# Attention units in pairs on TensorE, and both softmaxes of a pair scaled at the head of the next step

## The chip, the cores and the metric

One core of one Trainium2 chip. The metric is the device time of one execution of the program in microseconds; the table of the profile section gives it for the kernel before.

## What is computed

From the reference, cut to the core:

```python
def _attn_ref(q, k, v):            # (4, 8, 576, 64): batch, heads, positions, head size
    scores = scale * np.matmul(q, k.transpose(0, 1, 3, 2))
    ...                            
    scores = np.where(masks, scores, -1e9)   # heads 0-3: the last 32 positions; heads 4-7: every 4th of the last 128
    attn = np.exp(scores - np.max(scores, axis=-1, keepdims=True))
    attn = attn / (np.sum(attn, axis=-1, keepdims=True) + 1e-09)
    return np.matmul(attn, v)

def reference(**kwargs):
    x = attention output as (2304 tokens, 512)
    h = x @ w_in                   # (512, 2048)
    r = np.maximum(h, 0.0)
    x = (s * (r * r) + b) @ w_out  # (2048, 512)
    h = x @ moe2_w_in
    return (h * np.cos(h)) @ moe2_w_out
```

## The kernel before

The 2304 tokens are cut into five tiles of 384, 384, 512, 512 and 512 tokens. Each tile goes through the first MLP and later through the second. The loop at L539 counts steps p: 16 steps for each tile and MLP (one chunk of 128 of the 2048 hidden channels each), 160 in all. In step p, `mm_in` (L317) makes the hidden chunk h(p) on TensorE, `relu2` (L385) or `cos1` to `cos_split` turn it into g(p) on ScalarE and VectorE, and `mm_out` (L334) adds g(p-2) of an earlier step into the four outputs y. Tile 0 of the first MLP uses plain fp32 weights; every other tile uses each operand as a high and a low part, three matmuls of the rounded type in place of one.

Attention runs in 48 units (192 positions of two heads each; `dil` units have 4 blocks of 80 keys, plain ones 3 blocks of 96). Eight units (tile 0) run ahead of the loop. The other 40 run inside the steps of the first MLP, one tile ahead of the one that needs them: units 8 to 15 in steps 3 to 14, 16 to 27 in steps 15 to 30, 28 to 39 in steps 31 to 46, 40 to 47 in steps 48 to 62. A unit has five stations:

- `a_scores` (L211): 3 or 4 matmuls (`sc`) into one PSUM bank,
- `a_softmax` (L227): on VectorE scale and mask (L236) and the row maximum (L245), then on ScalarE 3 or 4 exponentials with their sums (L248),
- `a_norm` (L254): on VectorE 1/sum (L259, L260) and the scaling of the weights (L261),
- `a_transpose` (L263): transposes on TensorE (`tp`), copied to SBUF by ScalarE (L271),
- `a_pv` (L274): 6 or 8 small matmuls with v (`pv`), copied to the MLP's input by ScalarE (L299).

The order of all engines is written by hand (`manual_schedule`): every engine does its instructions in the order in which the loop records them. `at((p, phase), f)` puts a station into step p: phase 0 stands right behind `mm_in`, phases 1 and 2 at the step's end. Of each unit, with p counting one unit a step in most steps:

```python
at((p, 0), lambda i=i: a_scores(i, ps_a))
at((p, 1), lambda i=i: a_softmax(i))
at((p + 1, 0), lambda i=i: a_norm(i))
at((p + 2, 2), lambda i=i: a_transpose(i, ps_a, nc.scalar.copy))
at((p + 4, 0), lambda i=i: a_pv(i, ps_a))
```

h, sc, tp and pv share four PSUM banks in turn (pool `ps_a`): each waits until the tile four places earlier in that order has been read. The tiles of q and k, of v, and the softmax tiles have two buffers each.

In the same steps both MLPs' weights are prepared. `w_float` on ScalarE (L115, L116) and `w_join` on VectorE (four operations, L122 to L131) turn a chunk of 64-bit words into fp32: two chunks a step in steps 0 to 14 for the first MLP, and from step 19 on some 4, 8 and 10 chunks a tile for the second (`at((p, ph), ...)` at L517 to L532), each followed by `w_cut` (L141) one step later. `w_split` (L133) makes the high and low parts of the first MLP's weights, two a step in steps 16 to 28. Loads are issued from SyncE's queue, in the order of the program.

Of the kernel before, what the change touches and what calls it, by code (L numbers as in the profile page):

```python
# [26 lines left out]
NTILE = len(SIZES)  # L27
T = max(SIZES)
NCC = DM // P
NFC = DFF // P  # L30
LAG = (2, 3)
W_FIRST, W_STEPS = (7, 8, 9, 10), {8: 1, 9: 2, 11: 3}
V_LATE = 3
AHEAD = 3
WPRE, W_PACE = 4, 2.0
IN_CUT = 13

# [15 lines left out]
def attention_then_two_mlps(ctx, tc, qk_p, qk_d, v_p, v_d, mask_p, mask_d, w1, w2, sv, bv, out):  # L53
    nc = tc.nc
# [9 lines left out]
    ps_a = pool("ps_a", 4, space=PSUM)  # L64
# [13 lines left out]
    def xy_tile(t):  # L78

        if t not in xy:  # L80
            place = late[0] if t == 2 else xypool
            xy[t] = place.tile([P, NCC, T], F32, tag=f"xy{t % 3}", name=f"xy{t}")[:, :, : SIZES[t]]
        return xy[t]
# [87 lines left out]
    units = [(tb, hp) for b in blocks for hp in range(4) for tb in b]  # L171
    first_unit = [4 * sum(len(b) for b in blocks[:t]) for t in range(NTILE + 1)]
# [22 lines left out]
    def a_load(i):  # L195
        tb, hp = units[i]
        b, u = divmod(tb, 3)
        dil = hp >= 2
        nb, nq, nk = (4, DB, DK) if dil else (3, PB, PK)
        kw = nb * nk if dil else 3 * PB + WINDOW  # L200
        qk = io.tile([P, 384 + kw], F32, tag="qk", name=f"qk{i}")
        nc.sync.dma_start(qk, (qk_d if dil else qk_p)[b, hp % 2, u])
        st[i] = dict(q=qk[:, :384], k=qk[:, 384:], dil=dil, nb=nb, nq=nq, nk=nk, tb=tb, hp=hp, b=b, u=u)

    def a_load_v(i):
        d = st[i]
        vv = iov.tile([d["nk"], d["nb"], P], F32, tag="v", name=f"v{i}")
        nc.sync.dma_start(vv, (v_d if d["dil"] else v_p)[d["b"], d["hp"] % 2, d["u"]])
        d["v"] = vv

    def a_scores(i, ps):  # L211
        d = st[i]
        nb, nq, nk, dil = d["nb"], d["nq"], d["nk"], d["dil"]
        nr = 2 * nq
        acc = ps.tile([P, 512], F32, tag=ps_tag[ps.name], name=f"sc{i}")
        for j in range(nb):
            k0 = j * nk if dil else j * PB
            nc.tensor.matmul(  # L218
                acc[:nr, j * nk : (j + 1) * nk],
                d["q"][:, j * nr : (j + 1) * nr],  # L220
                d["k"][:, k0 : k0 + nk],
                start=True,
                stop=True,
            )
        d["acc"] = acc

    def a_softmax(i):  # L227
        d = st[i]
        nb, nq, nk, dil, acc = d["nb"], d["nq"], d["nk"], d["dil"], d.pop("acc")
        nr = 2 * nq  # L230
        sm = d["place"](3, [nr, nb, nk]) if "place" in d else ap_.tile([nr, nb, nk], F32, tag="sm", name=f"sm{i}")
        if dil:
            mask = m_d[:, (0 if d["u"] == 0 else 1) : (1 if d["u"] == 0 else 2), :].to_broadcast([nr, nb, nk])
        else:
            mask = m_p if d["u"] == 0 else m_p[:, 1:2, :].to_broadcast([nr, nb, nk])
        nc.vector.scalar_tensor_tensor(  # L236
            out=sm,
            in0=acc[:nr, : nb * nk].rearrange("p (j k) -> p j k", j=nb),
            scalar=1.0 / math.sqrt(D),
            in1=mask,  # L240
            op0=ALU.mult,
            op1=ALU.add,
        )
        nmax = ap_.tile([nr, nb], F32, tag="nmax", name=f"nmax{i}")
        nc.vector.tensor_reduce(out=nmax, in_=sm, op=ALU.max, axis=AX.X, negate=True)  # L245
        ssum = ap_.tile([nr, nb], F32, tag="ssum", name=f"ssum{i}")
        for j in range(nb):
            nc.scalar.activation(  # L248
                out=sm[:, j, :], in_=sm[:, j, :], func=AF.Exp, bias=nmax[:, j : j + 1], scale=1.0,
                accum_out=ssum[:, j : j + 1],  # L250
            )
        d["sm"], d["ssum"] = sm, ssum

    def a_norm(i):  # L254
        d = st[i]
        nb, nq, nk = d["nb"], d["nq"], d["nk"]
        nr = 2 * nq
        rec = ap_.tile([nr, nb, 1], F32, tag="rec", name=f"rec{i}")
        nc.vector.tensor_scalar_add(d["ssum"], d["ssum"], 1e-9)  # L259
        nc.vector.reciprocal(out=rec[:, :, 0], in_=d["ssum"])  # L260
        nc.vector.tensor_tensor(out=d["sm"], in0=d["sm"], in1=rec.to_broadcast([nr, nb, nk]), op=ALU.mult)  # L261

    def a_transpose(i, ps, copy=None):  # L263
        d = st[i]
        nb, nq, nk = d["nb"], d["nq"], d["nk"]
        nr = 2 * nq
        acc = ps.tile([P, 512], F32, tag=ps_tag[ps.name], name=f"tp{i}")
        for j in range(nb):
            nc.tensor.transpose(acc[:nk, j * nr : (j + 1) * nr], d["sm"][:, j, :], ident[:nr, :nr])  # L269
        pt = d["place"](4, [nk, 384]) if "place" in d else ap_.tile([nk, 384], F32, tag="pt", name=f"pt{i}")  # L270
        (copy or nc.vector.tensor_copy)(pt, acc[:nk, :384])  # L271
        d["pt"] = pt

    def a_pv(i, ps, tag=None):  # L274
        d = st.pop(i)
        nb, nq, nk, tb, hp = d["nb"], d["nq"], d["nk"], d["tb"], d["hp"]
        acc = ps.tile([P, 512], F32, tag=tag or ps_tag[ps.name], name=f"pv{i}")
        for j in range(nb):
            for h in range(2):
                c0 = (2 * j + h) * nq  # L280
                nc.tensor.matmul(  # L281
                    acc[h * D : (h + 1) * D, j * nq : (j + 1) * nq],
                    d["v"][:, j, h * D : (h + 1) * D],
                    d["pt"][:, c0 : c0 + nq],
                    start=True,
                    stop=True,
                )
        for t in range(NTILE):
            lo, hi = max(STARTS[t], tb * UB), min(STARTS[t + 1], tb * UB + UB)
            if lo >= hi:  # L290
                continue
            dst = xy_tile(t)[:, hp, lo - STARTS[t] : hi - STARTS[t]]
            lo, hi = lo - tb * UB, hi - tb * UB
            if d["dil"]:
                dst = dst.rearrange("p (i c) -> p c i", c=DIL)
                src = acc[:, :UB].rearrange("p (c i) -> p c i", c=DIL)[:, :, lo // DIL : hi // DIL]
            else:
                src = acc[:, lo:hi]
            nc.scalar.copy(dst, src)  # L299
# [129 lines left out]
    with tc.manual_schedule():  # L429
        n0 = 8  # L430
# [3 lines left out]
        def w_load_to(n):  # L434
            while wq[0] < min(n, 2 * NFC):
                w_load(0, wq[0], stage.tile([P, DM], I64, tag=f"s{wq[0] % 5}", name=f"stage{wq[0]}"))
                wq[0] += 1

        def w_whole(n):
# [3 lines left out]
            while q[2] < n:  # L443
# [5 lines left out]
                q[2] += 1  # L449
            w_load_to(q[2] + 1 + AHEAD)  # L450

# [4 lines left out]
        for i in range(1, n0 + V_LATE):  # L456
# [8 lines left out]
                nc.sync.dma_start(b_sb, bv.to_broadcast([P, 1]))  # L465
            if i in W_FIRST:
                w_load_to(wq[0] + 1)
        a_load(n0)
        a_load(n0 + 1)
        for k in range(n0 + 4):  # L470
            if k < n0:
                a_scores(k, ps_a)
# [13 lines left out]
        def at(slot, f):  # L486
            events.setdefault(slot, []).append(f)

        for i in range(n0, len(units)):
            t = next(t for t in range(NTILE) if i < first_unit[t + 1])  # L490
            n, j = first_unit[t + 1] - first_unit[t], i - first_unit[t]
            p = (t - 1) * NFC + (((3, 4, 5, 6, 7, 8, 9, 10) if t == 1 else (0, 1, 3, 4, 6, 8, 9, 10))[j] if n == 8 else j - 1)
            at((p, 0), lambda i=i: a_scores(i, ps_a))
            at((p + 1, 1), lambda i=i: a_load_v(i))
            if i + 2 < len(units):
                at((p, 0), lambda i=i: a_load(i + 2))
            at((p, 1), lambda i=i: a_softmax(i))
            at((p + 1, 0), lambda i=i: a_norm(i))
            at((p + 2, 2), lambda i=i: a_transpose(i, ps_a, nc.scalar.copy))
            at((p + 4, 0), lambda i=i: a_pv(i, ps_a))  # L500
        NP = 2 * NTILE * NFC

        def where(p):
            m, r = divmod(p, NTILE * NFC)
            t, fc = divmod(r, NFC)
            return m, t, fc
# [11 lines left out]
        for t, n in enumerate(BG):  # L518
            for i in range(n):
                b = t * NFC + (2 if t == 1 else 0) + (i + 0.5) * (NFC - (2 if t == 1 else 0)) / n  # L520
                p, ph = int(b), 1 + int(b % 1 >= 0.5)
# [17 lines left out]
        for p in range(NP + LAG[1]):  # L539
            if p < NP:  # L540
                m, t, fc = where(p)
# [133 lines left out]
```

## Time and profile before

| | |
|---|---|
| median of 3 runs | 934.41 us (932.59 to 934.5) |
| the profiled execution | 934.18 us, of which its span is 932.4 us |
| TensorE matmul busy | 906.8 us (97%) |
| VectorE busy | 590.2 us (63%) |
| ScalarE busy | 503.0 us (54%) |
| mean granted TensorE clock | 0.987 of full speed |
| median time to landing: q and k of a unit, v of a unit | 3.1 to 3.4 us, 2.5 to 2.7 us |

A step is read from the start of its first h matmul to that of the next step's. Steps 3 to 15 stand between 43.43 and 133.12 us of the span, steps 16 to 31 (tile 1) between 133.12 and 231.71, steps 32 to 47 (tile 2) between 231.71 and 339.16, steps 48 to 63 (tile 3) between 339.16 and 441.20. No attention is left behind that. "Idle before" in a row is time in which the engine had nothing to do, with the work that ended it. Matmuls are pipelined: what one group costs is read from its start to the start of the next.

### The profile page before, as it was taken

How to read it: one execution, taken by the hardware profiler on the slowest of the kernel's cores; microseconds unless marked ns; L12 is line 12 of the kernel's file. 1: busy time of each engine (PE TensorE's matmuls, PEld its weight loads, DVE VectorE, ACT ScalarE, POOL GpSimd, SP SyncE). 2: the span in 40 equal slices, each digit the busy share in tenths (PEclk: the TensorE clock that was granted, in tenths of full speed). 3: DMA queues.
4: the chain of work that ended last, by engine and by line, in shares of the span. 5: the costliest groups of instructions: out<-in, count | busy, mean ns of one | idle time of the engine just before them, and what ended most of it. 6: DMA issues, size and time to landing. Idle time of an engine off the chain costs nothing.

```text
span 932.4 us, 13282 instructions
## 1 busy us (share of the span) xinstructions
PE 906.8 (97%) x4888; PEld 758.3 (81%) x4888; DVE 590.2 (63%) x1160; ACT 503.0 (54%) x1162; POOL 0.7 (0%) x6
## 2 busy tenths in 40 slices
PE   6898999999999999999999999999999999999998
PEld 5555568889888788888888899999988888888886
DVE  6877876666665466665555676666665665566554
ACT  5756756666555555455443554554544554455443
POOL 0000000000000000000000000000000000000000
PEclk9799999999999999999999999999999999999999
DMA  9665514332454335426699810000000010001001
GB/s 259 231 236 172 195 39 133 113 109 74 147 165 155 127 104 175 136 84 215 226 322 303 279 63 1 1 34 1 2 33 1 0 46 1 1 1 46 0 1 46
DMA packets 45536, 99.64 MB, mean 107 GB/s; under 512 B 5440, under 2 KB 12064, under 8 KB 45472
## 3 DMA queue, kind: packets, MB, share of 16 engines
q1 hardware_dynamic: 45472, 98.80, 32.0%
q8 instruction: 39, 0.64, 0.3%
q14 instruction: 25, 0.20, 0.1%
HBM read 75.71 MB, written 23.07 MB: 106 GB/s over the span
## 4 chain that ended last, share of the span: by engine, by line
PE 83%; DVE 10%; ACT 5%; issue 1%; DMA 0%; SPq 0%; DVEq 0%; ACTq 0%
PE y L347 13%; PE y L349 12%; PE y L348 12%; PE h L330 12%; PE h L332 12%; PE h L331 12%; PE sc L218 2%; ACT sm L248 2%; PE pv L281 2%; PE h L324 2%; PE y L344 2%; DVE wa L131 1%; DVE wa L128 1%; DVE nmax L245 1%; PE tp L269 1%
## 5 line engine op out<-in xcount | busy, mean ns | idle before, releaser
L347 PE MATMUL y<-g,wh 128*128 128x512 f32 (+1 forms) x576 | 218.8, 380 | 0.0
L330 PE MATMUL h<-xs,wh 128*128 128x512 f32 (+1 forms) x576 | 217.4, 377 | 0.6 <-ACT pt L271 0.6
L349 PE MATMUL y<-g,wl 128*128 128x512 f32 (+1 forms) x576 | 214.9, 373 | 0.0
L348 PE MATMUL y<-g,wh 128*128 128x512 f32 (+1 forms) x576 | 214.7, 373 | 0.0
L332 PE MATMUL h<-xs,wl 128*128 128x512 f32 (+1 forms) x576 | 214.2, 372 | 0.0
L331 PE MATMUL h<-xs,wh 128*128 128x512 f32 (+1 forms) x576 | 213.9, 371 | 0.0
L347 PEld LDWEIGHTS y<-g,wh 128*128 128x128 f32 x576 | 109.1, 189 | 15.0
L349 PEld LDWEIGHTS y<-g,wl 128*128 128x128 f32 x576 | 108.7, 189 | 15.3
L330 PEld LDWEIGHTS h<-xs,wh 128*128 128x128 f32 x576 | 108.2, 188 | 15.6 <-ACT pt L271 0.8
L348 PEld LDWEIGHTS y<-g,wh 128*128 128x128 f32 x576 | 109.0, 189 | 14.4
L332 PEld LDWEIGHTS h<-xs,wl 128*128 128x128 f32 x576 | 108.1, 188 | 15.3
L331 PEld LDWEIGHTS h<-xs,wh 128*128 128x128 f32 x576 | 108.3, 188 | 14.8
L248 ACT ACTIVATE sm<-sm,nmax 96x80 f32<-96x80 f32 (+1 forms) x140 | 49.8, 357 | 104.3 <-DVE nmax L245 102.2
L414 ACT ACTIVATE n<-n 128x512 f32<-128x512 f32 (+1 forms) x80 | 47.2, 590 | 102.4 <-DVE n L408 102.3
L404 ACT ACTIVATE n<-h,pmagic 128x512 f32<-128x512 f32 (+1 forms) x80 | 51.6, 645 | 87.0 <-PE h L332 86.9
L405 DVE TENSOR_SCALAR n<-n 128x512 f32<-128x512 f32 (+1 forms) x80 | 32.0, 400 | 86.4 <-ACT n L404 86.4
L420 DVE SCALAR_TENSOR_TENSOR n<-n,h 128x512 f32<-128x512 f32 (+1 forms) x80 | 50.6, 633 | 55.2 <-ACT n L415 55.2
L388 ACT ACTIVATE r<-h 128x512 f32<-128x512 f32 (+1 forms) x80 | 44.6, 557 | 31.4 <-PE h L332 25.9
L398 DVE CAST g<-r 128x512 fp32r<-128x512 f32 (+1 forms) x64 | 26.1, 407 | 50.0 <-ACT r L396 49.9
L122 DVE TENSOR_SCALAR wa<-wa 128x512 f32<-128x512 f32 x62 | 26.2, 422 | 47.2 <-ACT wa L115 42.1
L408 DVE SCALAR_TENSOR_TENSOR n<-n,r 128x512 f32<-128x512 f32 (+1 forms) x80 | 51.1, 638 | 2.8
L407 DVE SCALAR_TENSOR_TENSOR r<-n,h 128x512 f32<-128x512 f32 (+1 forms) x80 | 50.7, 634 | 2.8
(81 smaller groups left out, 1084.4 us busy)
## 6 DMA issues: line engine op xcount, KB each, us to landing
stage<-w SPq DMA_DIRECT2D x32, 512.0 KB, 3.6
raw<-w SPq DMA_DIRECT2D x32, 512.0 KB, 4.5
cut<-raw SPq DMA_DIRECT2D x32, 256.0 KB, 2.3
cut<-wa SPq DMA_DIRECT2D x32, 256.0 KB, 2.6
wh<-cut SPq DMA_DIRECT2D x32, 256.0 KB, 3.6
wl<-cut SPq DMA_DIRECT2D x32, 256.0 KB, 4.1
qk<-qk_d SPq DMA_DIRECT2D x20, 352.0 KB, 3.4
qk<-qk_p SPq DMA_DIRECT2D x20, 304.0 KB, 3.1
```

The costliest lines, as they stand in the source:

```text
L248: nc.scalar.activation(out=sm[:, j, :], in_=sm[:, j, :], func=AF.Exp, bias=nmax[:, j : j + 1], scale=1.0, accum_out=ssum[:, j : j + 1],)
L330: nc.tensor.matmul(h[:, : SIZES[t]], hi, x[:, 0, :], start=cc == 0, stop=False)
L331: nc.tensor.matmul(h[:, : SIZES[t]], hi, x[:, 1, :], start=False, stop=False)
L332: nc.tensor.matmul(h[:, : SIZES[t]], lo, x[:, 0, :], start=False, stop=cc == NCC - 1)
L347: nc.tensor.matmul(y[:, : SIZES[t]], hi, g[:, 0, :], start=fc == 0, stop=False)
L348: nc.tensor.matmul(y[:, : SIZES[t]], hi, g[:, 1, :], start=False, stop=False)
L349: nc.tensor.matmul(y[:, : SIZES[t]], lo, g[:, 0, :], start=False, stop=fc == NFC - 1)
L404: nc.scalar.activation(out=n, in_=h[:, : SIZES[t]], func=AF.Identity, scale=1.0 / TWO_PI, bias=pmagic)
L407: nc.vector.scalar_tensor_tensor(out=r, in0=n, scalar=-C1, in1=h[:, : SIZES[t]], op0=ALU.mult, op1=ALU.add)
L408: nc.vector.scalar_tensor_tensor(out=n, in0=n, scalar=-C2, in1=r, op0=ALU.mult, op1=ALU.add)
L414: nc.scalar.activation(out=r, in_=r, func=AF.Sin, scale=0.5)
L420: nc.vector.scalar_tensor_tensor(out=r, in0=r, scalar=-1.0, in1=h[:, : SIZES[t]], op0=ALU.add, op1=ALU.mult)
```

## The change

The 40 units go through the stations as 20 pairs. A table `DUO` names the steps, tile by tile, at which a pair begins: two score groups stand behind each other, then two softmaxes; at the head of the next step both scalings; at that step's end both transposes; and at the end of the step behind it both products with v. So a pair's transposes stand one step after its scores (two before), its products with v two steps after (four before). The q and k loads of the next pair are issued with a pair's scores, its v loads behind a pair's products; those of units 8 and 9 ahead of the loop. The arithmetic is the same.

```diff
+DUO = ((), (3, 6, 9, 12), (0, 2, 5, 7, 10, 12), (0, 2, 5, 7, 10, 12), (1, 4, 8, 11))
...
-        a_load(n0)
-        a_load(n0 + 1)
+        for i in (n0, n0 + 1):
+            a_load(i)
+            a_load_v(i)
...
-        for i in range(n0, len(units)):
-            t = next(t for t in range(NTILE) if i < first_unit[t + 1])
-            n, j = first_unit[t + 1] - first_unit[t], i - first_unit[t]
-            p = (t - 1) * NFC + (((3, 4, 5, 6, 7, 8, 9, 10) if t == 1 else (0, 1, 3, 4, 6, 8, 9, 10))[j] if n == 8 else j - 1)
-            at((p, 0), lambda i=i: a_scores(i, ps_a))
-            at((p + 1, 1), lambda i=i: a_load_v(i))
-            if i + 2 < len(units):
-                at((p, 0), lambda i=i: a_load(i + 2))
-            at((p, 1), lambda i=i: a_softmax(i))
-            at((p + 1, 0), lambda i=i: a_norm(i))
-            at((p + 2, 2), lambda i=i: a_transpose(i, ps_a, nc.scalar.copy))
-            at((p + 4, 0), lambda i=i: a_pv(i, ps_a))
+        begin = [(t - 1) * NFC + s for t in range(1, NTILE) for s in DUO[t]]
+        duos = [(n0 + 2 * d, n0 + 2 * d + 1) for d in range(len(begin))]
+        assert duos[-1][1] == len(units) - 1
+        for d, (p, two) in enumerate(zip(begin, duos)):
+            later = duos[d + 1] if d + 1 < len(duos) else ()
+            for i in two:
+                at((p, 0), lambda i=i: a_scores(i, ps_a))
+                at((p, 1), lambda i=i: a_softmax(i))
+                at((p + 1, 0), lambda i=i: a_norm(i))
+                at((p + 1, 2), lambda i=i: a_transpose(i, ps_a, nc.scalar.copy))
+                at((p + 2, 2), lambda i=i: a_pv(i, ps_a))
+            for i in later:
+                at((p, 0), lambda i=i: a_load(i))
+                at((p + 2, 2), lambda i=i: a_load_v(i))
```

The changed file has two more lines ahead of this code, so its lines up to here are two higher.

TensorE in tile 0, from the transposes of unit 8 to its products with v (names carry the unit's or the step's number, `h0_0_6` is h of step 6). Before:

```order
L269 MATMUL tp8_701<-ident_92,sm8_593 96x128 x3
L324 MATMUL h0_0_6_707<-xy0_271,wa0_12_616 128x384 x4
L218 MATMUL sc11_716<-qk11_614 128x96 x3
L344 MATMUL y0_0_0_540<-g1_509,wa0_9_548 128x385
L344 MATMUL y0_0_1_541<-g1_509,wa0_9_548 128x385
L344 MATMUL y0_0_2_542<-g1_509,wa0_9_548 128x385
L344 MATMUL y0_0_3_543<-g1_509,wa0_9_548 128x385
L269 MATMUL tp9_757<-ident_92,sm9_643 96x128 x3
L324 MATMUL h0_0_7_763<-xy0_271,wa0_14_666 128x384 x4
L281 MATMUL pv8_768<-pt8_705,v8_641 64x64 x6
```

After:

```order
L271 MATMUL tp8_657<-ident_92,sm8_603 96x128 x3
L271 MATMUL tp9_663<-ident_92,sm9_611 96x128 x3
L326 MATMUL h0_0_5_669<-xy0_275,wa0_10_578 128x384 x4
L346 MATMUL y0_0_0_544<-g0_485,wa0_7_516 128x385
L346 MATMUL y0_0_1_545<-g0_485,wa0_7_516 128x385
L346 MATMUL y0_0_2_546<-g0_485,wa0_7_516 128x385
L346 MATMUL y0_0_3_547<-g0_485,wa0_7_516 128x385
L283 MATMUL pv8_699<-pt8_661,v8_172 64x64 x6
L283 MATMUL pv9_708<-pt9_667,v9_176 64x64 x6
L326 MATMUL h0_0_6_720<-xy0_275,wa0_12_632 128x384 x4
```

Before, the scores of unit 11, the transposes of unit 9 and a step's h and y stand between the transposes of unit 8 and its products; now one h and one y do, units 8 and 9 stand side by side, and all of it comes a step earlier.

VectorE in tile 0, from the softmax of unit 8 to the joins of weight chunks 11 and 12 (`wa0_11`, `wa0_12`). Before:

```order
L236 SCALAR_TENSOR_TENSOR sm8_593<-sc8_562,m_p_97 128x288
L245 TENSOR_REDUCE nmax8_595<-sm8_593 128x3
L259 TENSOR_SCALAR ssum8_597<-ssum8_597 128x3
L260 RECIPROCAL rec8_606<-ssum8_597 128x3
L261 TENSOR_TENSOR sm8_593<-sm8_593,rec8_606 128x288
L122 TENSOR_SCALAR wa0_11_584<-wa0_11_584 128x512
L125 TENSOR_SCALAR wa0_11_584<-wa0_11_584 128x512
L128 SCALAR_TENSOR_TENSOR wa0_11_584<-stage11_533,wa0_11_584 128x512
L131 ISA wa0_11_584<-stage11_533,wa0_11_584 128x1024
L122 TENSOR_SCALAR wa0_12_616<-wa0_12_616 128x512
```

After:

```order
L238 SCALAR_TENSOR_TENSOR sm8_603<-sc8_566,m_p_97 128x288
L247 TENSOR_REDUCE nmax8_605<-sm8_603 128x3
L238 SCALAR_TENSOR_TENSOR sm9_611<-sc9_570,m_p_97 128x288
L247 TENSOR_REDUCE nmax9_613<-sm9_611 128x3
L261 TENSOR_SCALAR ssum8_607<-ssum8_607 128x3
L262 RECIPROCAL rec8_624<-ssum8_607 128x3
L263 TENSOR_TENSOR sm8_603<-sm8_603,rec8_624 128x288
L261 TENSOR_SCALAR ssum9_615<-ssum9_615 128x3
L262 RECIPROCAL rec9_628<-ssum9_615 128x3
L263 TENSOR_TENSOR sm9_611<-sm9_611,rec9_628 128x288
L124 TENSOR_SCALAR wa0_11_594<-wa0_11_594 128x512
L127 TENSOR_SCALAR wa0_11_594<-wa0_11_594 128x512
```

The joins of chunks 11 and 12 stood between the scaling of unit 8 and the mask of unit 9; now the mask and maximum of unit 9 stand ahead of the scaling of unit 8, and the joins behind both scalings.

VectorE in tile 1, at one of the joins for the second MLP (`wa1_1`, `wa1_2`) that stands between a softmax and its scaling. Before:

```order
L236 SCALAR_TENSOR_TENSOR sm24_1805<-sc24_1770,m_d_98 96x320
L245 TENSOR_REDUCE nmax24_1807<-sm24_1805 96x4
L122 TENSOR_SCALAR wa1_1_1814<-wa1_1_1814 128x512
L125 TENSOR_SCALAR wa1_1_1814<-wa1_1_1814 128x512
L128 SCALAR_TENSOR_TENSOR wa1_1_1814<-raw1_1737,wa1_1_1814 128x512
L131 ISA wa1_1_1814<-raw1_1737,wa1_1_1814 128x1024
L259 TENSOR_SCALAR ssum24_1809<-ssum24_1809 96x4
L260 RECIPROCAL rec24_1850<-ssum24_1809 96x4
L261 TENSOR_TENSOR sm24_1805<-sm24_1805,rec24_1850 96x320
L138 TENSOR_TENSOR wl0_22_1862<-wa0_22_920,wh0_22_1861 128x512
```

After, behind the mask and maximum of unit 24:

```order
L238 SCALAR_TENSOR_TENSOR sm25_1999<-sc25_1955,m_d_98 96x320
L247 TENSOR_REDUCE nmax25_2001<-sm25_1999 96x4
L124 TENSOR_SCALAR wa1_2_2008<-wa1_2_2008 128x512
L127 TENSOR_SCALAR wa1_2_2008<-wa1_2_2008 128x512
L130 SCALAR_TENSOR_TENSOR wa1_2_2008<-raw2_1935,wa1_2_2008 128x512
L133 ISA wa1_2_2008<-raw2_1935,wa1_2_2008 128x1024
L261 TENSOR_SCALAR ssum24_1994<-ssum24_1994 96x4
L262 RECIPROCAL rec24_2028<-ssum24_1994 96x4
L263 TENSOR_TENSOR sm24_1990<-sm24_1990,rec24_2028 96x320
L261 TENSOR_SCALAR ssum25_2003<-ssum25_2003 96x4
L262 RECIPROCAL rec25_2032<-ssum25_2003 96x4
L263 TENSOR_TENSOR sm25_1999<-sm25_1999,rec25_2032 96x320
```

The join stood between the maximum of one unit and its scaling; now the scalings of two units stand behind it. In tile 1 this is so for pairs 22/23 and 24/25, in tile 2 for 32/33 and 34/35, in tile 3 for 42/43 and 44/45.

## Rows read from the trace of the kernel before

**Rows 1.** Busy times by stretch: steps 3-15, 16-31, 32-47, 48-63; columns below.

```profile
core 0: us, PE busy (x) PEld busy (x) DVE busy (x) ACT busy (x) POOL busy (x), PEclk, DMA share, GB/s
43.43:133.12 89.69, 84.30 (x412) 51.62 (x410) 70.71 (x148) 58.39 (x158) 0.00 (x0) 0.98 0.49 170
133.12:231.71 98.59, 93.72 (x672) 86.14 (x671) 64.07 (x144) 61.84 (x185) 0.00 (x0) 0.97 0.33 105
231.71:339.16 107.45, 107.45 (x673) 87.51 (x673) 63.35 (x139) 58.53 (x172) 0.00 (x0) 1.00 0.45 143
339.16:441.20 102.04, 102.04 (x582) 83.00 (x580) 62.94 (x129) 56.56 (x142) 0.00 (x0) 1.00 0.43 141
```

**Rows 2.** The same view for single steps: 3, 37, 67 and 84.

```profile
43.43:49.27 5.84, 5.84 (x23) 3.71 (x22) 5.29 (x11) 4.37 (x8) 0.00 (x0) 1.00 0.71 256
263.98:271.21 7.23, 7.23 (x50) 5.81 (x48) 4.84 (x13) 3.46 (x12) 0.00 (x0) 1.00 0.35 106
457.52:462.96 5.44, 5.44 (x26) 4.50 (x24) 3.27 (x7) 1.74 (x3) 0.00 (x0) 1.00 0.74 251
548.40:552.56 4.16, 4.16 (x26) 4.16 (x26) 2.58 (x6) 2.03 (x4) 0.00 (x0) 1.00 0.00 0
```

**Rows 3.** Timeline of PE in tile 0: start, us, operation, [idle before, releaser].

```profile
46.01 0.80 PE L218 MATMUL sc<-qk 128*128 128x96 f32 x6
46.65 2.78 PE L344 MATMUL y<-g,wa 128*128 128x385 f32 x8
...
74.99 0.90 PE L218 MATMUL sc<-qk 128*96 128x80 f32 x8 [2.17 <-DVE sm L236]
```

**Rows 4.** Timeline of DVE in tile 0: a plain and a dil unit.

```profile
51.69 0.45 DVE L236 SCALAR_TENSOR_TENSOR sm<-sc,m_p 128x288 f32<-128x288 f32 x1
...
53.87 0.17 DVE L259 TENSOR_SCALAR ssum<-ssum 128x3 f32<-128x3 f32 x1 [1.25 <-ACT sm L248]
...
54.66 0.42 DVE L122 TENSOR_SCALAR wa<-wa 128x512 f32<-128x512 f32 x1
...
82.12 0.48 DVE L236 SCALAR_TENSOR_TENSOR sm<-sc,m_d 96x320 f32<-96x320 f32 x1
...
84.73 0.17 DVE L259 TENSOR_SCALAR ssum<-ssum 96x4 f32<-96x4 f32 x1 [1.61 <-ACT sm L248]
...
85.55 0.42 DVE L122 TENSOR_SCALAR wa<-wa 128x512 f32<-128x512 f32 x1
```

**Rows 5.** Timeline of DVE in tile 1: two masks, and a join behind one.

```profile
180.21 0.48 DVE L236 SCALAR_TENSOR_TENSOR sm<-sc,m_d 96x320 f32<-96x320 f32 x1
...
186.34 0.48 DVE L236 SCALAR_TENSOR_TENSOR sm<-sc,m_d 96x320 f32<-96x320 f32 x1
...
189.51 0.43 DVE L122 TENSOR_SCALAR wa<-wa 128x512 f32<-128x512 f32 x1 [2.17 <-ACT wa L115]
...
191.87 0.16 DVE L259 TENSOR_SCALAR ssum<-ssum 96x4 f32<-96x4 f32 x1
```

**Rows 6.** Timeline of PE in tile 1: scores behind a wait.

```profile
195.29 1.52 PE L218 MATMUL sc<-qk 128*96 128x80 f32 x8 [1.56 <-DVE sm L236]
```

**Rows 7.** Timeline of PE in tile 2: products, scores and transposes between h and y.

```profile
252.49 0.57 PE L281 MATMUL pv<-pt,v 96*64 96x64 f32 x12
252.99 0.91 PE L218 MATMUL sc<-qk 128*128 128x96 f32 x6
253.68 0.48 PE L347 MATMUL y<-g,wh 128*128 128x512 f32 x1
...
256.52 0.49 PE L269 MATMUL tp<-ident,sm 128*96 128x128 f32 x3
256.76 0.47 PE L330 MATMUL h<-xs,wh 128*128 128x512 f32 x1
```

**Rows 8.** Timelines at the start of tile 1, ACT: relu behind h of step 16.

```profile
135.79 0.49 ACT L388 ACTIVATE r<-h 128x384 f32<-128x384 f32 x1 [2.12 <-PE h L332]
```

**Rows 9.** The same place on DVE: mask of that step's unit.

```profile
138.34 0.45 DVE L236 SCALAR_TENSOR_TENSOR sm<-sc,m_p 128x288 f32<-128x288 f32 x1
```

## The prediction

> **What bounds the kernel now.** I read the busy times by stretch first [rows 1]. In steps 32 to 63 TensorE is busy for the whole of each stretch; in steps 3 to 15 and 16 to 31 it is idle for 5.4 and 4.9 us, and its mean granted clock is 0.98 and 0.97 of 2.4 GHz. Behind 441.2 us nothing changes. So the change can win in two ways: less idle time in the first two stretches, and cheaper attention groups on TensorE in all four.
>
> Then single steps [rows 2]. A step without attention lasts 5.44 us at 512 tokens and 4.16 at 384; one with a whole unit lasts 7.23, so **a unit costs TensorE 1.79 us**. In tile 0 a step with scores alone lasts 5.84, and the scores take 0.64 of it (46.01 to 46.65 [rows 3]), so the plain step is 5.20. This gives what each stretch would last with nothing waiting:
> - A, steps 3 to 15: 13 x 5.20 + 8 x 1.79 + one more score group 0.7 = 82.6 us; measured 89.7.
> - B, steps 16 to 31: 14 x 4.16, two steps with one half of tile 0's kind at 4.68, and 12 x 1.79 = 89.1; measured 98.6.
> - C, steps 32 to 47: 14 x 5.44, two mixed steps at 4.80, 12 units less one score group = 106.5; measured 107.45.
> - D, steps 48 to 63: 16 x 5.44 + 8 x 1.79 = 101.4; measured 102.0.
>
> So A holds 7.1 us of waits and slow clock, B 9.5, C and D 0.9 and 0.6.
>
> Third, who makes TensorE wait. In A the scores wait 2.17 us for the mask of an earlier unit, which holds their bank [rows 3]. VectorE's chain of one unit in A is mask, maximum, wait for the exponentials, scaling: 51.69 to 54.66 = 2.97 us for a plain unit, 82.12 to 85.55 = 3.43 for a dil one, with 1.25 and 1.61 us of waiting in it [rows 4]. Two joins a step come on top, 2.36 us each (189.51 to 191.87 [rows 5]). That is 7.7 to 8.2 us a step against TensorE's 5.20 + 1.79 = 6.99. VectorE is the bound there, and TensorE falls into waits at the banks. In B the masks of successive units stand 6.13 us apart [rows 5] against TensorE's 4.16 + 1.79 = 5.95: ScalarE waits for VectorE and VectorE for ScalarE once each per unit, and together they are slower than TensorE. A join behind a mask adds more: 186.34 to 191.87 before the scaling may start, where the plain wait would have ended 2.6 us after the mask.
>
> **The change, part by part.**
>
> *TensorE's groups.* Products, scores and transposes of one unit take 0.50, 0.69 and 0.24 us [rows 7], 1.43 of the 1.79. The other 0.36 belongs to two interruptions of the MLP (products with scores, transposes), 0.18 each. A pair needs three interruptions (scores, transposes, products) where two units had four: 0.18 saved. Scores that follow products take 0.69, scores that follow h took 0.64 [rows 3]: 2 x 0.05 saved. That is 0.28 a pair, **5.6 us** for 20 pairs. No row shows two groups of the same kind side by side, so its ends are 0 and 0.36 + 0.10 a pair (9.2 us). The rows show weight loads hidden under matmuls: in step 84 the loads are busy for all of the 4.16 us that the matmuls are [rows 2]. The Trainium skill (TensorE: Matmul & The Clock Gate, Part 3: Packing small matmuls) says that a weight load overlaps with running matmuls only where the row groups differ. By that rule a group would pay for its loads wherever it stands, and this term would be 0; the trace disagrees for the large matmuls, which all use the same 128 rows.
>
> *VectorE's chain of a pair.* Masks and maxima of two plain units take 2 x 0.93 (51.69 to 52.62, where the wait of 1.25 begins). The first unit's sums are there at 0.93 + 1.25 = 2.18, its scaling lasts 0.79 (53.87 to 54.66 [rows 4]) to 2.97. One more exponential costs 1.61 - 1.25 = 0.36, so the second unit's three follow 1.08 later, at 3.26, and its scaling ends at **4.05 us instead of 2 x 2.97**. A dil pair: 3.43 + 4 x 0.36 = 4.87 instead of 6.86. In A VectorE then needs for three steps 4.05 + 6 x 2.36 = 18.2 us (dil 19.0), TensorE 3 x 5.20 + 2 x 1.79 - 0.28 = 18.9: about even, where VectorE was over by 0.7 to 1.2 a step. The waits of A go, but with little to spare. Worked through: the first mask stays at 51.69, since VectorE's order is the same up to it; its pair is scaled at 55.74. TensorE arrives at the transposes at 46.01 + 1.28 + 2.62 + 5.20 = 55.1, the second group 0.3 later, so 0.4 us of wait. The later pairs find their scalings done by 0.1 to 1 us. A after: 67.6 + 14.3 - 1.1 + 0.4 = 81.2, which is **8.5 less**.
>
> *Transposes one step after the scores.* This is the new risk. The mask comes 2.55 us after the relu, which begins when h is out [rows 8, 9]; a group is out about 0.2 us after TensorE has begun the next one (252.99 + 0.91 against 253.68 [rows 7]). So counted from TensorE's last h matmul the mask starts at 2.8, a plain pair is scaled at 2.8 + 4.05 = 6.9 us, a dil pair at 7.7. TensorE arrives at the transposes after two score groups, y, h and y: 1.4 + 3 x 2.08 + 0.2 = 7.8 in B and 9.8 in C and D. So pairs without a join just pass in B. With a join between, the join starts at 3.17 (186.34 to 189.51 [rows 5]) + 1.44 for the second unit's four exponentials, lasts 2.36, and two scalings of 0.8 follow: 8.6 after the mask, 11.4 after h. In B pair 24/25 waits 11.4 - 8.0 = 3.4 us (second group), pair 22/23, which has the products of 20/21 ahead of it (1.2 us), 2.0. In C 32/33 waits some 0.6 and 34/35 0.2, in D 42/43 0.6 and 44/45 1.4.
>
> A wait of 1.56 us was followed by scores of 1.52 us [rows 6] instead of 0.90 [rows 3], the clock being at 1.2 GHz for a while: a mean of 0.97 over 98.6 us is 3.0 us lost [rows 1], and I put it on two such places in B, 1.5 each. I add 1.5 for one of the two waits in B.
>
> B after: 89.1 - 1.7 + 5.4 + 1.5, and 0.9 for what even C did not explain = 95.2, **3.4 less**. C after, with a whole score group back that B had: 106.5 + 0.7 - 1.7 + 0.8 + 0.9 = 107.2, **0.2 less**. D after: 101.4 - 1.1 + 2.0 + 0.6 = 102.9, **0.9 more**.
>
> *Banks.* The tile that waits closest is h of the step after the next score pair's step: it takes the bank of the pair's first scores or products, read by then in the order above (mask at 2.8 + 0.5, h at 1.4 + 2.1 after h, if no products stand between). In B that leaves 0.2 us; it is counted in the 0.9.
>
> *Loads.* On SyncE's queue the q and k loads wait for the scores of the pair ahead and are issued two or three steps before use, over 8 us; the v loads wait for products at a step's end, with one weight load at most behind them, which is used a step later. Both land in time; if not, scores would show a DMA as releaser. ScalarE and VectorE have the same instructions as before. Where the second MLP's work begins, everything is as it was.
>
> **Sum:** 8.5 + 3.4 + 0.2 - 0.9 = 11.2 us. The profiled execution took 934.18 (0.2 below the median), so 923.0.
>
> **Rivals.**
> - *Pairing saves nothing on TensorE.* The gain is 11.2 - 5.6 = 5.6: 928.6. For it: the only neighbours of plain fp32 groups in the trace, scores behind products, are slower, not faster [rows 7]. The Trainium skill's rule above (Part 3 of its TensorE page) would give this, and the trace bears it out only so far.
> - *The joins cost nothing.* If the pair chains with a join are ready in time, because VectorE runs ahead in the longer gaps, B, C and D give back 5.4 + 1.5 + 0.8 + 2.0 = 9.7: 913.3. Against it: the join waits for ScalarE's floats, which stand behind eight exponentials.
> - *Slower: the chains of a pair run one after the other.* If the second unit's exponentials are held up (by ScalarE's relu, casts and copies between, as in B now), a pair takes 5.94 or 6.86 instead of 4.05 or 4.87. In C and D the 2 to 3 us of room cover it. In the ten pairs of A and B it is 1.9 late each with 0.1 to 0.8 of room, some 16 us, and six waits over 1.5 us with 1.5 of slow clock each, 9 more: 923 + 25 = 948. It decides from 1.1 us a pair on (11.2 over ten).
> - *The scaling is not moved at all:* it stood at the head of the next step for single units already; what changes is that two stand there. So if the transposes had kept their place, only A and the groups would gain. This is part of the sum, not a case of its own.
>
> **Chances.** The forecast (919 to 927) 0.52, pairing without a saving on TensorE 0.20, free joins 0.13, the late chains 0.10, and 0.05 that the losses of B to D eat the gain of A, about 934. Two-tenths of a per cent (1.9 us) is about what can be told from no change. Faster 0.85, the same 0.05, slower 0.10. The range 913 to 931 takes in both ends of the TensorE term (919.4 and 928.6), the free joins and twice the joins' waits; it leaves out the late chains and no change.
>
> **What would show it.** Right: in A no wait of scores for a mask; TensorE at the h of step 16 some 8 us earlier; second transposes waiting for a scaling in pairs 22/23, 24/25 and 44/45, and nowhere else by over 1 us; a pair of product groups within 1.05 us. Wrong: transposes waiting in most pairs of A and B, a clock under 0.97 in B, scores or products released by a DMA, or a pair of groups that takes as long as two apart.

## The result and the profile after

The changed kernel takes 926.15 us (median of 4 runs, 924.52 to 926.42); the kernel before took 933.5 in the same comparison. The ratio is 0.991, with a 95% interval of 0.989 to 0.9931. The profiled execution took 924.52 us; the other three (926.0 to 926.4) had a mean granted clock of 0.986 where it had 0.990.

The busy times by the same four stretches of steps as [rows 1], in the profile of the changed kernel (length, then busy time of each engine, then the mean granted clock):

```profile
42.92:123.12 80.20, 79.83 (x405) 50.40 (x404) 70.33 (x147) 58.41 (x152) 0.00 (x0) 1.00 0.55 187
123.12:217.88 94.76, 89.52 (x673) 84.19 (x671) 65.19 (x147) 63.67 (x189) 0.00 (x0) 0.98 0.34 110
217.88:324.45 106.57, 106.10 (x679) 88.37 (x679) 62.38 (x138) 60.31 (x173) 0.00 (x0) 1.00 0.45 146
324.45:431.55 107.10, 102.61 (x582) 83.90 (x581) 63.00 (x129) 57.74 (x142) 0.00 (x0) 0.98 0.39 133
```

VectorE and ScalarE do the same work as before. Stretch A became 9.5 us shorter and TensorE has almost no idle time in it; B is 3.8 shorter, C 0.9. But D, where TensorE never waited before, is 5.1 us **longer**, idle for 4.5 us and at a clock of 0.98. That takes back over a third of the 14.2 us that A, B and C gave. Behind D both kernels run alike (491.20 us before, 491.15 after, to the end of the span).

Which waits are left on TensorE in these steps, in the view of waits (in total, times, longest):

```profile
PE tp L271 <- DVE ssum L261: 8.2, 4, 2.8
PE tp L271 <- DVE sm L263: 2.0, 7, 0.4
```

Scores no longer wait for a mask, as in [rows 3, 6]: there is no such line. Transposes wait for the scalings instead, which the kernel before has no line for. The places stand in the timeline of TensorE (start, length, operation, idle before):

```profile
55.46 0.51 PE L271 MATMUL tp<-ident,sm 128*96 128x128 f32 x3 [0.37 <-DVE sm L263]
174.47 0.50 PE L271 MATMUL tp<-ident,sm 96*80 96x96 f32 x4 [1.77 <-DVE ssum L261]
175.29 0.50 PE L271 MATMUL tp<-ident,sm 96*80 96x96 f32 x4 [0.32 <-DVE sm L263]
193.81 0.50 PE L271 MATMUL tp<-ident,sm 96*80 96x96 f32 x4 [2.84 <-DVE ssum L261]
194.62 0.77 PE L271 MATMUL tp<-ident,sm 96*80 96x96 f32 x4 [0.31 <-DVE sm L263]
263.43 0.51 PE L271 MATMUL tp<-ident,sm 128*96 128x128 f32 x3 [0.28 <-DVE sm L263]
344.63 0.62 PE L271 MATMUL tp<-ident,sm 128*96 128x128 f32 x3 [2.35 <-DVE ssum L261]
345.42 0.85 PE L271 MATMUL tp<-ident,sm 128*96 128x128 f32 x3 [0.17 <-DVE sm L263]
366.93 0.50 PE L271 MATMUL tp<-ident,sm 128*96 128x128 f32 x3 [0.28 <-DVE sm L263]
392.97 0.50 PE L271 MATMUL tp<-ident,sm 96*80 96x96 f32 x4 [1.29 <-DVE ssum L261]
393.79 0.50 PE L271 MATMUL tp<-ident,sm 96*80 96x96 f32 x4 [0.32 <-DVE sm L263]
```

In order: the first pair of tile 0; pairs 22/23 and 24/25 in tile 1; 32/33 in tile 2; and in tile 3 pairs 40/41, 42/43 and 44/45. All but the first and 40/41 are pairs that have a weight chunk's joins between softmax and scaling. Where a pair waits for joins, most of the wait stands ahead of its first transposes; the prediction put it ahead of the second.

The chain of a plain pair on VectorE, first pair of tile 0 (answers to [rows 4], where one unit took 2.97 us):

```profile
51.18 0.45 DVE L238 SCALAR_TENSOR_TENSOR sm<-sc,m_p 128x288 f32<-128x288 f32 x1
...
53.37 0.17 DVE L261 TENSOR_SCALAR ssum<-ssum 128x3 f32<-128x3 f32 x1 [0.40 <-ACT sm L250]
...
54.44 0.17 DVE L261 TENSOR_SCALAR ssum<-ssum 128x3 f32<-128x3 f32 x1 [0.20 <-ACT sm L250]
...
55.23 0.42 DVE L124 TENSOR_SCALAR wa<-wa 128x512 f32<-128x512 f32 x1
```

From 51.18 to 55.23 it takes 4.05 us for two units, with 0.60 us of waiting in place of 2 x 1.25: while ScalarE works on the exponentials of one unit, VectorE masks the other.

### The profile page after: what moved, and what is told of

Its sections match the earlier page's. It is cut to its first block, busy times and chain, and to the rows that moved or that the text cites. A ratio compares the mean times of both kernels' runs of the same rounds, so it can differ in the third digit from the quotient of the medians.

```text
span 922.7 us, 13285 instructions
## 1 busy us (share of the span) xinstructions
PE 895.6 (97%) x4888; PEld 755.4 (82%) x4888; DVE 590.2 (64%) x1160; ACT 507.5 (55%) x1162; POOL 0.7 (0%) x6
## 4 chain that ended last, share of the span: by engine, by line
PE 88%; DVE 7%; ACT 3%; issue 1%; DMA 0%; SPq 0%; DVEq 0%
PE h L332 13%; PE h L333 13%; PE h L334 13%; PE y L349 12%; PE y L350 12%; PE y L351 12%; PE y L346 4%; PE h L326 4%; PE sc L220 2%; PE pv L283 2%; ACT sm L250 2%; PE tp L271 1%; DVE wa L133 1%; DVE wa L130 1%; DVE nmax L247 1%
## 5 line engine op out<-in xcount | busy, mean ns | idle before, releaser
L349 PE MATMUL y<-g,wh 128*128 128x512 f32 (+1 forms) x576 | 214.9, 373 | 0.0
L350 PE MATMUL y<-g,wh 128*128 128x512 f32 (+1 forms) x576 | 213.6, 371 | 0.0
```

The source lines that it names most:

```text
L349: nc.tensor.matmul(y[:, : SIZES[t]], hi, g[:, 0, :], start=fc == 0, stop=False)
L350: nc.tensor.matmul(y[:, : SIZES[t]], hi, g[:, 1, :], start=False, stop=False)
```

## The experiments

The theory behind the prediction: VectorE's chain, shortened by pairing, is what A gains; the transposes one step after the scores are what the later tiles pay, where something stands between softmax and scaling; TensorE's groups become a little cheaper. The rivals: the gain comes from spreading units over more steps; the joins cost their time wherever they stand; the groups on TensorE cost the same wherever they stand.

**Pairs in tile 0 only.** Units 16 to 47 keep their old steps:

```diff
+        begin, duos = begin[:4], duos[:4]
+        for i in range(duos[-1][1] + 1, len(units)):
+            ...
+            p = (t - 1) * NFC + ((0, 1, 3, 4, 6, 8, 9, 10)[j] if n == 8 else j - 1)
+            at((p, 0), lambda i=i: a_scores(i, ps_a))
+            ...
```

> Pairs in tile 0 only (units 8 to 15); the other 32 units one at a time at their steps of before. My theory: tile 0 is where VectorE was the bound, and 10 us of the 9.7 that the changed kernel gains stand at its end; tiles 1 to 3 give about as much as they lose: 924 to 926 us. Rival (the gain of tile 0 is given back when the later tiles start earlier, and what counts is the groups on TensorE): 929 to 932.

Measured: 924.01 us (ratio 0.9896, 0.9882 to 0.991). Stretch A of its profile:

```profile
42.83:123.69 80.86, 80.48 (x411) 51.05 (x410) 70.68 (x148) 59.03 (x158) 0.00 (x0) 1.00 0.54 185
```

Tile 0 alone gives the whole gain, and 2 us more than the whole change in the medians (0.5 in the profiled executions). So the 32 units behind it lose as much as they win, and a little over.

**Spread without pairs.** One unit at a time, in two successive steps where the pair had one, the stations as close to each other as in the change:

```diff
-        begin = [(t - 1) * NFC + s for t in range(1, NTILE) for s in DUO[t]]
...
+        SOLO = ((), (3, 4, 6, 7, 9, 10, 11, 12), (0, 1, 2, 3, 5, 6, 7, 8, 9, 10, 11, 12), (0, 1, 2, 3, 5, 6, 7, 8, 9, 10, 11, 12), (1, 2, 4, 5, 8, 9, 11, 12))
+        begin = [(t - 1) * NFC + s for t in range(1, NTILE) for s in SOLO[t]]
+        for d, p in enumerate(begin):
+            i = n0 + d
+            at((p, 0), lambda i=i: a_scores(i, ps_a))
+            at((p, 1), lambda i=i: a_softmax(i))
+            at((p + 1, 0), lambda i=i: a_norm(i))
+            at((p + 1, 2), lambda i=i: a_transpose(i, ps_a, nc.scalar.copy))
+            at((p + 2, 2), lambda i=i: a_pv(i, ps_a))
...
```

> Pairing undone, spreading kept: one unit at a time, in about the same steps as the pairs (a unit in each of two successive steps), stations as far apart as in the changed kernel. My theory: in tile 0 the chains of two units take 2 x 2.97 or 2 x 3.43 us of VectorE again, 1.2 to 1.9 us over what TensorE leaves per pair, and TensorE's extra interruptions come back (about 0.3 us a pair): 932 to 938 us. Rival (the gain comes from spreading the units over more steps and from fewer steps between stations): 924 to 928.

Measured: 936.73 us (ratio 1.0033, 1.0019 to 1.0047), slower than before. Its stretch A, then VectorE's chain of one unit there, and two of the waits:

```profile
43.63:130.64 87.01, 81.65 (x406) 50.19 (x404) 70.22 (x147) 57.73 (x152) 0.00 (x0) 1.00 0.50 172
```

```profile
71.76 0.45 DVE L238 SCALAR_TENSOR_TENSOR sm<-sc,m_p 128x288 f32<-128x288 f32 x1
...
73.95 0.17 DVE L261 TENSOR_SCALAR ssum<-ssum 128x3 f32<-128x3 f32 x1 [1.25 <-ACT sm L250]
...
74.74 0.42 DVE L124 TENSOR_SCALAR wa<-wa 128x512 f32<-128x512 f32 x1
```

```profile
62.03 0.57 PE L283 MATMUL pv<-pt,v 96*64 96x64 f32 x12 [1.07 <-ACT pt L273]
...
163.18 0.50 PE L271 MATMUL tp<-ident,sm 128*96 128x128 f32 x3 [3.22 <-DVE sm L263]
```

One unit holds VectorE for 2.98 us again, so two hold it for 5.96 in place of 4.05, A lasts 6.8 us longer with VectorE and ScalarE about as busy, and transposes and products wait. Against the kernel before, A is 2.7 us shorter (87.0 against 89.7, at a clock of 1.00 in place of 0.98), where the pairs made it 9.5 shorter. So spreading and bringing the stations closer give a small part of A's gain without pairing, and nothing over the whole kernel; the rival falls. In tiles 1 to 3 this run also changes which joins meet which unit, so only A separates the causes cleanly.

**Joins moved out of the pairs.** The chunk's load and cut move along with its joins:

```diff
                 p, ph = int(b), 1 + int(b % 1 >= 0.5)
+                if p in begin:
+                    p += 1
```

> The changed kernel, but a weight chunk of the second MLP whose floats and joins would stand in a pair's first step (between that pair's softmax and scaling) has them one step later. My theory: the second transposes of pairs 22/23, 24/25, 32/33, 42/43 and 44/45 wait because the join stands ahead of their scalings; in the changed kernel these waits sum to 7.4 us, with one or two slow stretches of the clock behind them. They should go: 917 to 920 us against 926. Rival (the join costs VectorE and ScalarE its time wherever it stands, and the waits turn up elsewhere): 925 to 927.

Measured: 916.57 us (ratio 0.9819, 0.9806 to 0.9831), 9.6 less than the changed kernel and a little under the range. Its waits on TensorE's transposes are now those of the first pair, of 40/41 and one new one:

```profile
202.76 0.50 PE L271 MATMUL tp<-ident,sm 96*80 96x96 f32 x4 [1.66 <-DVE ssum L261]
203.57 0.50 PE L271 MATMUL tp<-ident,sm 96*80 96x96 f32 x4 [0.31 <-DVE sm L263]
339.18 1.63 PE L271 MATMUL tp<-ident,sm 128*96 128x128 f32 x6 [2.35 <-DVE ssum L261]
```

The new one (pair 26/27) comes from the move: the cut of the moved chunk, one step behind its joins, now stands between that pair's softmax and scaling. On VectorE it waits 3.18 us for its cast on ScalarE, and the scalings stand behind it:

```profile
201.12 0.69 DVE L148 TENSOR_TENSOR wa<-wa,raw 128x512 fp32r<-128x512 f32 x1 [3.18 <-ACT raw L147]
```

The joins themselves cost nothing where no scaling stands behind them.

**The first pair of tile 3 moved as well.**

```diff
-DUO = (..., (1, 4, 8, 11))
+DUO = (..., (2, 5, 8, 11))
```

> As the run before, and the four pairs of the last tile begin at its steps 2, 5, 8 and 11 instead of 1, 4, 8 and 11. My theory: pair 40/41 waited 2.5 us in its transposes because its softmax stood behind the copies of the finished tile's output in the same step, with about 1.9 us of slow clock behind it; moved one step on it has them out of its way: 4 us less than the run before, 913 to 916 us. Rival (the pair's chain is too long for this tile anyway): the same time as the run before, within 1 us.

Measured: 911.1 us (ratio 0.9755, 0.9743 to 0.9768), 5.5 less than the run before it and under the range. Of these D explains 4.3 (104.4 to 100.1 us in the two profiles); in the profiles the first h of step 3 also began 1.2 us earlier (42.66 against 43.84), ahead of anything that was changed. What the pair met in the changed kernel shows in ScalarE's and VectorE's timelines of step 49:

```profile
334.85 0.78 ACT L362 ACTIVATE xy<-y,bsum,s_sb 128x512 f32<-128x512 f32 x1 [4.51 <-PE y L351]
336.21 0.78 ACT L362 ACTIVATE xy<-y,bsum,s_sb 128x512 f32<-128x512 f32 x1 [0.58 <-PE y L351]
336.89 0.59 ACT L390 ACTIVATE r<-h 128x512 f32<-128x512 f32 x1
...
342.38 0.60 ACT L147 CAST raw<-wa 128x512 fp32r<-128x512 f32 x1
```

```profile
339.24 0.45 DVE L238 SCALAR_TENSOR_TENSOR sm<-sc,m_p 128x288 f32<-128x288 f32 x1
...
343.01 0.69 DVE L148 TENSOR_TENSOR wa<-wa,raw 128x512 fp32r<-128x512 f32 x1 [1.98 <-ACT raw L147]
...
345.19 0.42 DVE L400 CAST g<-r 128x512 fp32r<-128x512 f32 x1
```

In that step the output y of tile 2 is finished, and its copies stand ahead of the relu on ScalarE. They wait 4.5 us for y, so relu begins at 336.89, and the mask behind it at 339.24, when TensorE has already gone through y.

A second thing stands in the way of this pair, which my theory left out: the cut of the chunk whose joins stand in step 48. Its cast on ScalarE (342.38) follows the pair's six exponentials, and VectorE waits 1.98 us for it at 343.01, ahead of both scalings. So the pair holds VectorE for 5.95 us (339.24 to 345.19), where the first pair of tile 0 takes 4.05. The move takes the pair away from the late mask and from the cut at once; no run separates the two.

TensorE waits 2.35 + 0.17 us in the transposes at 344.6, and the matmuls behind them run at 1.2 GHz for a while (granted clock 0.50 between 345.4 and 347.5; 0.63 us, where such a matmul takes 0.37 on average):

```profile
346.49 0.63 PE L333 MATMUL h<-xs,wh 128*128 128x512 f32 x1
```

**The last join moved.**

```diff
                 if p in begin:
                     p += 1
+                if t == 1 and i == 2:
+                    p = 29
```

> As the run with the moved joins and the moved first pair, and the third weight chunk of tile 1 has its joins in step 29, so that neither they nor the cut behind them stand between the softmax and the scaling of pair 26/27. My theory: the one wait left in the transposes of that run, 1.66 + 0.31 us in step 29, goes: 1.5 to 2.5 us less than its 911.1, 908.5 to 909.8 us. Rival (the wait moves to another step, since ScalarE now has two chunks to float there): 910.5 to 912.

Measured: 908.71 us (ratio 0.9732, 0.9719 to 0.9746), faster than the change by 17.4 us. The wait is gone and no other has come. Its four stretches:

```profile
43.71:123.89 80.18, 79.82 (x405) 50.40 (x404) 70.30 (x147) 58.41 (x152) 0.00 (x0) 1.00 0.56 187
123.89:211.11 87.22, 87.22 (x672) 82.71 (x671) 64.71 (x146) 63.02 (x189) 0.00 (x0) 1.00 0.36 119
211.11:316.59 105.48, 105.48 (x680) 88.48 (x679) 63.51 (x139) 60.84 (x175) 0.00 (x0) 1.00 0.46 146
316.59:416.68 100.09, 100.09 (x581) 83.19 (x580) 62.80 (x129) 56.92 (x141) 0.00 (x0) 1.00 0.43 145
```

TensorE is busy from end to end in B, C and D, at full clock. This is what the pairs give when no wait is left.

**Products apart.** The two product groups of a pair on either side of the step's y:

```diff
-                at((p + 2, 2), lambda i=i: a_pv(i, ps_a))
+                at((p + 2, 0 if i == two[0] else 2), lambda i=i: a_pv(i, ps_a))
```

> The changed kernel with the two product groups of a pair apart: the first unit's stands behind the h of its step, the second's stays at that step's end. Where the next pair begins in that step (6 of 20) the first unit's products join its scores, in the other 14 pairs TensorE has one interruption of the MLP more. My theory (an interruption costs about 0.18 us of its own): 14 x 0.18 = 2.5 us slower, 928 to 929 us against 926, and two product groups cost some 0.2 us more than as a pair in steps without waits. Rival (every group pays for its weight loads wherever it stands): the same as the changed kernel, within 1 us.

Measured: 937.38 us (ratio 1.0036, 1.0023 to 1.0049), 11.2 more than the changed kernel where I expected 2.5. The step with the products of pair 42/43, without waits, first in the changed kernel, then here:

```profile
367.19:373.67 6.48, 6.48 (x52) 5.19 (x49) 4.62 (x8) 3.09 (x6) 0.00 (x0) 1.00 0.40 138
```

```profile
376.38:383.28 6.90, 6.90 (x52) 5.19 (x49) 4.62 (x8) 3.07 (x6) 0.00 (x0) 1.00 0.45 154
```

With its products apart, a pair costs 0.42 us more in this step. Over the fourteen steps with a pair's products that have no wait in either kernel it is 0.29 to 0.42, in most some 0.35, twice the 0.18 that I had put down. It is so too where the first group stands beside scores and TensorE has no interruption more: step 34 went from 7.86 to 8.22 us. A part of it stands in the starts of the groups, first in the changed kernel, then here:

```profile
372.82 0.92 PE L283 MATMUL pv<-pt,v 96*64 96x64 f32 x24
373.67 0.50 PE L332 MATMUL h<-xs,wh 128*128 128x512 f32 x1
```

```profile
379.32 0.57 PE L283 MATMUL pv<-pt,v 96*64 96x64 f32 x12
379.82 0.50 PE L349 MATMUL y<-g,wh 128*128 128x512 f32 x1
```

Apart, a group takes 0.50 us to the start of the next matmul (the second too, 382.78 to 383.28); side by side the two take 0.85 together, 0.15 us less. The rest falls to the matmuls around the group. Some 0.35 over 20 pairs is 7 us; the rest are waits, of products for the copies of the transposes (1.6 us in 3 places) and of the transposes of pair 22/23 (2.69 us in place of 1.77), and a lower clock in B (0.97 in place of 0.98). So place matters on TensorE, more than I had said, and the rival that the groups cost the same wherever they stand falls.

**Scalings at the step's end.**

```diff
-                at((p + 1, 0), lambda i=i: a_norm(i))
+                at((p + 1, 1), lambda i=i: a_norm(i))
```

> The changed kernel with both scalings of a pair at the end of the step that follows the scores, behind that step's other work on VectorE, instead of at its head. My theory: at the head the scalings wait only for the exponentials; at the end they wait for the joins of two chunks in tile 0 (4.7 us a pair) and for the cast and the subtraction of that step's g behind its h in the other tiles, so the transposes wait 1 to 4 us in nearly every pair: 25 us or more over the changed kernel, 945 to 975 us. Rival (the place hardly matters, since the exponentials end last): within 3 us of the changed kernel.

Measured: 972.87 us (2 runs; ratio 1.0418, 1.0398 to 1.0437). The longest of its waits:

```profile
PE tp L271 <- DVE ssum L261: 39.6, 18, 4.9
```

In this schedule, transposes one step after the scores need the scalings at the head of that step. That place is not new for a single unit; how much it mattered there, with two steps to the transposes, was not run.

## Why the prediction was right, and where it was not

The range (913 to 931) held the time, and the change is faster as forecast, by 7.4 us in the medians. Against the profiled execution, against which the sum was made, it is 9.7 us where the sum said 11.2. That the two are so close is in part luck: D came out 4.2 us above its term, A, B and C together 2.0 below theirs, and 0.5 of the 9.7 arose ahead of step 3 (it begins at 43.43 before and 42.92 after, and between 42.6 and 43.8 over all runs). By stretches, in us; the last column is the version without waits:

| | before | sum | after | joins and pair moved |
|---|---|---|---|---|
| A, steps 3 to 15 | 89.7 | 81.2 | 80.2 | 80.2 |
| B, steps 16 to 31 | 98.6 | 95.2 | 94.8 | 87.2 |
| C, steps 32 to 47 | 107.45 | 107.2 | 106.6 | 105.5 |
| D, steps 48 to 63 | 102.0 | 102.9 | 107.1 | 100.1 |

- *VectorE's chain of a pair*, 4.05 us from the rows of single units: measured 4.05. The first pair's wait in the transposes, 0.4: measured 0.37. A is right to 1.0 us, and the runs with pairs in tile 0 alone and with spread single units show that pairing is the cause.
- *Waits behind a join*: 3.4 and 2.0 us for pairs 24/25 and 22/23, measured 3.15 and 2.09; 1.4 for 44/45, measured 1.61; 0.6 each for 32/33 and 42/43, measured 0.28; 0.2 for 34/35, which did not wait. The mechanism is shown by moving the joins.
- *The clock*: I put 1.5 us on one of B's waits. The mean of 0.98 over 94.8 us is 1.9. That D would have such a stretch I had not seen.
- *The step that failed* is in the part on transposes one step after the scores: "counted from TensorE's last h matmul the mask starts at 2.8". I read that 2.8 at one place and took it for all pairs. In step 49 the copies of the finished tile's y stand ahead of the relu, and the mask starts 3.8 us later (h ran from 329.89 to some 332.6, the mask began at 339.24: 6.6 us in place of 2.8). The order of the changed program showed that; in tiles 1 and 2 the pair begins one step before such copies, and I did not look at tile 3. The sum also put a chunk's cut between a pair's softmaxes and its scalings at nothing, and the chain of 40/41 with its cut lasts 5.95 us in place of 4.05. In the sum's own terms the pair is then scaled at 6.6 + 5.95 = 12.6 us after h, where TensorE comes at 9.8: a wait of 2.8, measured 2.52. By the same terms the late mask alone makes 0.9 and the cut alone nothing (8.8 against 9.8); this is an estimate, as no run separates them. The wait and the slow clock behind it are the 4.2 us by which D was too low.
- *TensorE's groups*: 0.28 a pair. In the version without waits D lasts 100.1 us, of which 16 x 5.44 is the MLP: 13.05 us for four pairs, 3.26 each, against 2 x 1.79: 0.32. The size was right but its split was not: no term had that a second product group beside its like takes 0.35 us where one alone takes 0.50, and products apart cost 0.35 in most steps, not 0.18. The prediction weighed the Trainium skill's rule on weight loads (TensorE: Matmul & The Clock Gate, Part 3: Packing small matmuls) and read it to mean that place would not matter; the run with products apart disagrees with that reading, with 6.90 against 6.48 us in a step.
- *The rivals*: no saving on TensorE is ruled out. Free joins was the other way round: the joins cost about what the sum said, and can be moved. The late chains did not come: in all 20 pairs the second unit's exponentials follow the first's without a gap.
- *The signs named ahead*: in A no scores wait for a mask, the first h of step 16 starts 10.0 us earlier where some 8 were forecast (123.12 against 133.12), and a pair of product groups takes 0.85 us, under the 1.05. That no transposes but those of 22/23, 24/25 and 44/45 would wait over 1 us did not hold, because of 40/41.

The median is 1.6 us above the profiled execution, with a mean clock of 0.986 in the other executions against 0.990; where their clock was lower was not profiled.

## What to carry to other kernels

Where two engines hand a chain to and fro, put two independent chains side by side: each engine works on one while the other waits, and the bound engine loses most of its waits without doing less (0.60 us in place of 2.50 a plain pair). Then go through every place of the new schedule and ask what stands between the stations on each engine's own queue: here six pairs of 20, with a chunk's preparation or a tile's output in between, took back well over half of what the others gave, and moving these few pieces by a step or three brought the gain from 7.4 to 24.9 us. A delay that was read at one place holds only for the steps that have the same work in front.

## What was not expected

A group of 12 to 16 small products away from its like cost 0.29 to 0.42 us more than the same group beside it (6.90 against 6.48 us in one step), and standing beside another kind of small matmul did not spare it (8.22 against 7.86). Two waits of 2.4 and 0.2 us cost the waits themselves and some 2 us of matmuls at 1.2 GHz behind them (D's mean clock of 0.98). The length of a wait alone does not tell whether that comes: behind a wait of 3.22 us in the run with spread single units the granted clock stayed at 1.00 (163.2 to 167.0), behind one of 1.56 us in the kernel before [rows 6] it was 0.50 (195.4 to 198.0).
